# Attention scores computed transposed, softmax between 32x32 block transposes, in a fused attention and MLP kernel

## The chip, the cores and the metric

One program runs on one core of a Trainium2 chip. The metric is the device time of one execution in microseconds; lower is better.

## What is computed

The reference chains three blocks: a linear attention through 32 memory slots, a token- and channel-mixing MLP, and a gated mixture of four attention experts. The change touches only the first block and its meeting with the second:

```python
a = exp(phi - max(phi, axis=2)); a = a / (sum(a, axis=2) + 1e-09)      # over the sequence
k_m = einsum('bhsm,bhsd->bhmd', a, k); v_m = einsum('bhsm,bhsd->bhmd', a, v)
scores = matmul(q, k_m.transpose(0, 1, 3, 2)) / sqrt(64)               # 576 queries x 32 slots
attn = exp(scores - max(scores, axis=-1)); attn = attn / (sum(attn, axis=-1) + 1e-09)
attn_out = matmul(attn, v_m)
# MLP: x = heads of attn_out side by side
h = maximum(x.T @ w_tok1, 0) @ w_tok2; u = x + h.T; out = u + maximum(u @ w_ch1, 0) @ w_ch2
```

Batch 8, 8 heads, 576 positions, head size 64, 32 slots. q and k are 64 times as large as v, which is part of the inputs' setup.

## The kernel before

The attention runs in 16 units; a unit is one batch element and four heads. Each unit passes through the steps `s1a` to `s4c`, and a loop over t (lines near 560) starts the steps of several units in each round: `s1a` of unit t+3, `s2k` of t+2, `s3`, `s3b` and `s3c` of t+1, `s4a`, `s4g`, `s4b` and `s4c` of t. Between the steps it puts pieces of the channel MLP (`b1some`, tiles `b`, `u`, `uh`, `ul`, `hh`, `hl`), which fill TensorE, and pieces of the weight preparation (`go`, tiles `cst`, `cm`, `cy`), which split float64 weights on DVE and ACT. From this program text a scheduler, which models the engines' times, makes the order of each engine's queue; each queue is then executed in order.

The steps around the change:

- `s2k` (L303, L309, L312) makes the slots' keys and values: float32 products in four column tiles of 32, tile `g`, from `kv` and `ea`. `s2q` (L359, L366) turns q on TensorE into `qTb`; `s2t` turns the keys into `kmT`.
- `s3` (L376 to L383) makes the scores, tile `s` in PSUM: queries on the partitions, 4 heads x 32 slots along the row, five blocks of 128 queries (the last one half empty). DVE takes the maximum of each 32 (`smx`, L379) and subtracts it (L382, into `ssb`), ACT takes the exponential (L383).
- `s3b` (L388 to L392) sums, inverts (`ssm`), and multiplies on POOL into `at`, queries on the partitions.
- `s3c` (L402 to L405) splits `at` into a rounded part and a rest (`ahi`, `alo`) for the products with two such parts; `s4g` uses them for the token mixing's first product (L98, L434, L435, `t1h`, `t1l`).
- `s4a` (L413, L415) turns `at` on TensorE so that heads and slots lie on the partitions, and splits it into `aT`; `s4c` (L471) multiplies that with the slots' values, and adds the token mixing.

Queries lie on the partitions in the order of the load, four neighbours to a partition, and the rows of `w_tok1` are loaded in the same order (`tok1`).

Of the kernel before, what the change touches and what calls it, by code (L numbers as in the profile page):

```python
# [62 lines left out]
def fused_kernel(ctx: ExitStack, tc, q, k, v, phi, w_tok1, w_tok2, w_ch1, w_ch2,  # L63
# [136 lines left out]
    with ExitStack() as sa:  # L200
# [20 lines left out]
        qTb = [ld.tile([128, 2, 640], F32, name=f"qTb{i}") for i in range(NB2)]  # L221
        for i in range(NB2):
            DVE.memset(phb[i][64:128, :, 4, :], NEG)
            DVE.memset(qTb[i][:, :, S:640], 0.0)
# [128 lines left out]
        def s2q(n, part):  # L353
            qn = qn_
            qT = qTb[n % NB2]
            if part < 2:
# [5 lines left out]
                ACT.activation(qT[:, part, 0:512], p3[:], AF.Copy)  # L362
# [8 lines left out]
        def s3(n):  # L371
            qT, km = qTb[n % NB2], kmT.pop(n)
            p = pp.tile([128, 5, 4, M], F32, name="s", bufs=1)
            for j in range(5):
                for pr in range(2):
                    PE.matmul(p[:, j, 2 * pr:2 * pr + 2, :], lhsT=qT[:, pr, 128 * j:128 * j + 128],  # L376
                              rhs=km[:, 64 * pr:64 * pr + 64], start=True, stop=True)
            mx = wk_.tile([128, 5, 4], F32, name="smx", bufs=1)
            DVE.tensor_reduce(mx[:], p[:], axis=AX.X, op=OP.max)  # L379
            s = wk_.tile([128, 5, 4, M], F32, name="ssb", bufs=1)  # L380
            ssb[n] = s
            DVE.tensor_sub(s[:], p[:], mx[:, :, :, None].to_broadcast([128, 5, 4, M]))  # L382
            ACT.activation(s[:], s[:], AF.Exp, scale=scale)  # L383

        def s3b(n):
            s = ssb.pop(n)
            sm = wk_.tile([128, 5, 4], F32, name="ssm", bufs=2)
# [3 lines left out]
            a_ = wk_.tile([128, 5, 128], F32, name="at", bufs=1)  # L391
            POOL.tensor_mul(a_[:].rearrange("p j (h m) -> p j h m", h=4), s[:],  # L392
                            sm[:, :, :, None].to_broadcast([128, 5, 4, M]))
            ah[n] = a_

        def s3c(n):
# [4 lines left out]

            ACT.activation(hi[:, 0:4, :], a_[:, 0:4, :], AF.Copy)  # L402
            ACT.activation(hi[0:ST, 4, :], a_[0:ST, 4, :], AF.Copy)
            POOL.tensor_sub(hi[ST:128, 4, :], a_[0:ST, 4, :], f(hi[0:ST, 4, :]))
            POOL.tensor_sub(lo[:], a_[:, 0:4, :], f(hi[:, 0:4, :]))  # L405

        def s4a(n):
            a_ = ah.pop(n)
            x_ = wk_.tile([128, 2, S], F32R, name="aT", bufs=2)
            aTt[n] = x_  # L410
            p = pp.tile([128, 512], F32, name="t", bufs=2)
            for j in range(4):
                PE.transpose(p[:, 128 * j:128 * j + 128], a_[:, j, :], ident[:])  # L413
            p2 = pp.tile([128, 128], F32, name="t", bufs=2)
            PE.transpose(p2[:], a_[:, 4, :], ident[:])  # L415

            for src, cs, j in ((p[:], slice(0, 512), 4), (p2[:, 0:ST], slice(512, S), 1)):
                if n < NR:
                    split(x_[:, 0, cs].rearrange("k (p j) -> k p j", j=j),
                          x_[:, 1, cs].rearrange("k (p j) -> k p j", j=j),  # L420
                          src.rearrange("k (j p) -> k p j", j=j))
                    continue
                for c, o in ((0, 0), (1, 64)):
                    sv = src[o:o + 64, :].rearrange("k (j p) -> k p j", j=j)
                    hv = x_[o:o + 64, c, cs].rearrange("k (p j) -> k p j", j=j)
                    lv = x_[64 - o:128 - o, c, cs].rearrange("k (p j) -> k p j", j=j)
                    split(hv, lv, sv)
# [54 lines left out]
        def tok1(j, n):  # L482
            s_ = stg.tile([128, S, 2], I32, name="cst", bufs=3)[:, 0:n * T, :]
            if j < 4:
                src = w1w[0:SM].rearrange("(p j) t -> p j t", j=4)[:, j:j + n, :]
# [885 lines left out]
```

## Time and profile before

| | us |
|---|---|
| median of 3 runs | 1220.99 |
| lowest and highest run | 1220.82, 1222.42 |
| span of the profiled execution, first to last instruction | 1219.0 |
| PE busy (97% of the span) | 1180.3 |
| PE weight loads busy (91%) | 1104.3 |
| DVE busy (67%) | 812.8 |
| ACT busy (51%) | 627.3 |
| POOL busy (35%) | 429.0 |

The page gives no time of the profiled execution other than its span; the median of the runs is 2.0 us above it. Matmuls are pipelined, so their busy times overlap, and the profile models their ends: how fast a row of matmuls runs is read from their starts. One float32 matmul appears as two passes, so an instruction of the program counts twice there. A unit's number in this document counts from 0 in the order of the program.

### The profile page before, as it was taken

How to read it: one execution, taken by the hardware profiler on the slowest of the kernel's cores; microseconds unless marked ns; L12 is line 12 of the kernel's file. 1: busy time of each engine (PE TensorE's matmuls, PEld its weight loads, DVE VectorE, ACT ScalarE, POOL GpSimd, SP SyncE). 2: the span in 40 equal slices, each digit the busy share in tenths (PEclk: the TensorE clock that was granted, in tenths of full speed). 3: DMA queues.
4: the chain of work that ended last, by engine and by line, in shares of the span. 5: the costliest groups of instructions: out<-in, count | busy, mean ns of one | idle time of the engine just before them, and what ended most of it. 6: DMA issues, size and time to landing. Idle time of an engine off the chain costs nothing.

```text
span 1219.0 us, 24055 instructions
## 1 busy us (share of the span) xinstructions
PE 1180.3 (97%) x8730; PEld 1104.3 (91%) x8730; DVE 812.8 (67%) x2013; ACT 627.3 (51%) x1651; POOL 429.0 (35%) x622
## 2 busy tenths in 40 slices
PE   5789999999999999999999999999999999999998
PEld 4689999999988889899999889999999899999986
DVE  6867778886575756667566513787676667777753
ACT  3555656566453323223222212777676766777774
POOL 1432435344001112112111344555454637373331
PEclk9699999999999999999999999999999999999999
DMA  9866767654283221232123343322323333322422
GB/s 242 228 183 179 216 163 217 189 151 118 79 295 102 104 70 35 70 104 79 61 70 104 97 112 113 87 84 79 83 87 83 88 109 91 101 84 67 149 85 104
DMA packets 160917, 145.09 MB, mean 119 GB/s; under 512 B 73248, under 2 KB 128800, under 8 KB 160800
## 3 DMA queue, kind: packets, MB, share of 16 engines
q1 hardware_dynamic: 160800, 143.57, 40.5%
q8 instruction: 69, 1.13, 0.4%
q14 instruction: 48, 0.39, 0.1%
HBM read 91.10 MB, written 40.89 MB: 108 GB/s over the span
## 4 chain that ended last, share of the span: by engine, by line
PE 89%; DVE 4%; DMA 4%; ACT 1%; SPq 1%; issue 1%; POOL 0%; ACTq 0%; DVEq 0%
PE g L98 30%; PE o L98 16%; PE h L98 15%; PE b L98 8%; PE y L1143 4%; PE s L1034 3%; PE t L1098 3%; PE s L376 2%; DMA cst<-in_moe_w_ch_dram 1%; PE g L303 1%; PE s L1056 1%; DMA cst<-in_moe_w_tok_dram 1%; PE t L359 1%; PE g L471 1%; PE t L98 1%
## 5 line engine op out<-in xcount | busy, mean ns | idle before, releaser
L1079 POOL TENSOR_TENSOR a<-a,cf 128x128 f32<-128x128 f32 (+3 forms) x128 | 88.2, 722 | 71.1 <-DVE cf L1071 70.9
L98 PE MATMUL o<-hl,w2h 128*128 128x512 f32 x288 | 112.6, 391 | 0.0
L98 PE MATMUL o<-hh,w2l 128*128 128x512 f32 x288 | 112.4, 390 | 0.0
L98 PE MATMUL o<-hh,w2h 128*128 128x512 f32 x288 | 107.9, 392 | 0.0
L649 ACT ACTIVATE hh<-m 128x256 fp32r<-128x256 f32 x96 | 38.9, 415 | 110.9 <-DVE m L720 71.3
L392 POOL TENSOR_TENSOR at<-ssb,ssm 128x640 f32<-128x640 f32 x16 | 21.5, 1343 | 173.7 <-DVE ks L319 82.1
L1023 DVE CUSTOM_DVE_ANT_0 ssb<-s,cmask 128x128 f32<-128x128 f32 (+2 forms) x144 | 68.3, 482 | 20.3 <-PE s L1034 13.1
L1036 ACT ACTIVATE a<-ssb,nb 128x128 f32<-128x128 f32 (+3 forms) x128 | 71.4, 558 | 20.2 <-DVE nb L1023 14.7
L650 DVE SCALAR_TENSOR_TENSOR hl<-m,hh 128x256 fp32r<-128x256 f32 x96 | 58.2, 616 | 17.6 <-ACT hh L649 15.5
L98 PE MATMUL g<-xh,qkl 128*128 128x288 f32 x232 | 68.4, 297 | 0.0
L98 PE MATMUL g<-xl,qkh 128*128 128x288 f32 x232 | 68.4, 297 | 0.0
L98 PE MATMUL g<-xh,qkh 128*128 128x288 f32 x232 | 68.1, 300 | 0.0
L98 PE MATMUL h<-ul,w1h 128*128 128x512 f32 (+2 forms) x200 | 66.9, 334 | 0.0
L98 PE MATMUL h<-uh,w1l 128*128 128x512 f32 (+2 forms) x200 | 66.8, 334 | 0.0
L98 PE MATMUL h<-uh,w1h 128*128 128x512 f32 (+2 forms) x200 | 66.5, 333 | 0.0
L697 POOL TENSOR_TENSOR tl<-ub,th 128x512 fp32r<-128x512 f32 x12 | 18.1, 1525 | 136.3 <-ACT th L696 136.3
L98 PEld LDWEIGHTS o<-hh,w2l 128*128 128x128 f32 x288 | 54.1, 188 | 11.4
L105 DVE TENSOR_TENSOR Bl<-t,Bh 128x512 fp32r<-128x512 f32 (+1 forms) x80 | 50.4, 634 | 20.8 <-ACT Bh L102 19.9
L98 PEld LDWEIGHTS o<-hh,w2h 128*128 128x128 f32 x288 | 54.0, 188 | 10.4 <-DVE pb L745 0.9
L932 POOL TENSOR_TENSOR xl<-p,xh 128x288 fp32r<-128x288 f32 x60 | 47.6, 812 | 44.1 <-ACT xh L931 44.1
L98 PEld LDWEIGHTS o<-hl,w2h 128*128 128x128 f32 x288 | 54.1, 188 | 9.4
L682 POOL TENSOR_TENSOR ub<-ub 128x512 f32<-128x512 f32 x6 | 9.7, 1619 | 131.0 <-DVE ul L105 131.0
(335 smaller groups left out, 4383.5 us busy)
## 6 DMA issues: line engine op xcount, KB each, us to landing
cst<-in_moe_w_ch_dram SPq DMA_DIRECT2D x24, 512.0 KB, 4.8
u_d<-u SPq DMA_DIRECT2D x32, 288.0 KB, 2.2
p_d<-u SPq DMA_DIRECT2D x16, 576.0 KB, 3.3
ub<-u_d SPq DMA_DIRECT2D x9, 1024.0 KB, 5.0
pb<-p_d SPq DMA_DIRECT2D x36, 256.0 KB, 3.9
x_d<-pb SPq DMA_DIRECT2D x36, 256.0 KB, 2.6
u<-u_d SPq DMA_DIRECT2D x16, 576.0 KB, 4.0
p<-x_d SPq DMA_DIRECT2D x15, 576.0 KB, 4.0
```

The costliest lines, as they stand in the source:

```text
L98: PE.matmul(ps, lhsT=a, rhs=b, start=start and i == 0, stop=stop and i == len(seq) - 1)
L105: DVE.tensor_sub(lo, src, f(hi))
L376: PE.matmul(p[:, j, 2 * pr:2 * pr + 2, :], lhsT=qT[:, pr, 128 * j:128 * j + 128], rhs=km[:, 64 * pr:64 * pr + 64], start=True, stop=True)
L649: ACT.activation(hh, c, AF.Relu)
L650: DVE.scalar_tensor_tensor(hl, c, 0.0, f(hh), op0=OP.max, op1=OP.subtract)
L932: POOL.tensor_sub(xl[b][:, c, ss], x_, f(xh[b][:, c, ss]))
L1023: DVE.tensor_tensor_reduce(out=out, in0=p, in1=mask, scale=-scale, scalar=least, op0=OP.add, op1=OP.min, accum_out=acc)
L1034: PE.matmul(p[:, 0:W], lhsT=q_[n][:, 128 * c:128 * c + 128], rhs=kk[n][:, 0:W], start=(i == 0), stop=(i == 1))
L1036: ACT.activation(a[:, aoff[c]:aoff[c] + W], s_[:, 0:W], AF.Exp, scale=-1.0, bias=nb[:, 0:1], accum_out=sm[:, c:c + 1])
L1079: POOL.tensor_mul(x_, x_, cf[:, c:c + 1].to_broadcast([128, W]))
L1098: PE.transpose(p[:, 128 * kc:128 * kc + 128], a[:, o + 128 * kc:o + 128 * kc + 128], ident[:])
L1143: PE.matmul(p[:, lo:w], lhsT=v_[:, kc, 0, :], rhs=x, start=(i == 0), stop=(i == len(ops) - 1))
```

## The change

- `s3` multiplies the other way round: the keys `kmT` are the weights and `qTb` streams, 512 queries and then 64, each for two pairs of heads in a column tile of 64. The scores stand with heads and slots on the partitions and queries along the row, 576 instead of 640.
- DVE transposes them in blocks of 32x32 from PSUM into `ssb`, which brings the 32 slots of a head and query into one row. DVE takes the maximum, POOL (not DVE) subtracts it in SBUF, ACT takes the exponential.
- `s3b` multiplies on POOL in place, and DVE transposes the blocks back into `at`, which now has heads and slots on the partitions.
- `s3c` turns `at` on TensorE to queries on the partitions (five transposes, the last with 64 columns) and splits it from PSUM, on ACT and DVE. `s4a` no longer turns anything; it splits `at` from SBUF, on ACT and POOL.
- `s2q` writes q in natural order, and the rows of `w_tok1` are loaded in natural order, in pieces of half the length. The padding of `qTb` and its memset go.

```diff
--- before.py
+++ after.py
@@ -218,10 +218,9 @@
             DVE.memset(kmask[32 * h:32 * h + 32, h % 2, :], 1.0)
         NB2 = 2
         phb = [ld.tile([128, 4, 5, M], F32, name=f"phb{i}") for i in range(NB2)]
-        qTb = [ld.tile([128, 2, 640], F32, name=f"qTb{i}") for i in range(NB2)]
+        qTb = [ld.tile([128, 2, S], F32, name=f"qTb{i}") for i in range(NB2)]
         for i in range(NB2):
             DVE.memset(phb[i][64:128, :, 4, :], NEG)
-            DVE.memset(qTb[i][:, :, S:640], 0.0)
         kv_ = ld.tile([128, 2, 4, 5, D], F32, name="kv")
         qn_ = ld.tile([128, 5, 4, D], F32, name="qn")
         DVE.memset(kv_[ST:128, :, :, 4, :], 0.0)
@@ -359,7 +358,8 @@
                     PE.transpose(p3[:, 128 * j:128 * j + 128],
                                  qn[:, j, 2 * part:2 * part + 2, :].rearrange("p h d -> p (h d)"),
                                  ident[:])
-                ACT.activation(qT[:, part, 0:512], p3[:], AF.Copy)
+                ACT.activation(qT[:, part, 0:512].rearrange("k (p j) -> k p j", j=4),
+                               p3[:].rearrange("k (j p) -> k p j", j=4), AF.Copy)
                 return
             p4 = pp.tile([128, 2, 128], F32, name="t", bufs=2)
             for pr in range(2):
@@ -370,27 +370,29 @@
 
         def s3(n):
             qT, km = qTb[n % NB2], kmT.pop(n)
-            p = pp.tile([128, 5, 4, M], F32, name="s", bufs=1)
-            for j in range(5):
+            p = pp.tile([128, S], F32, name="s", bufs=1)
+            for cs in (slice(0, 512), slice(512, S)):
                 for pr in range(2):
-                    PE.matmul(p[:, j, 2 * pr:2 * pr + 2, :], lhsT=qT[:, pr, 128 * j:128 * j + 128],
-                              rhs=km[:, 64 * pr:64 * pr + 64], start=True, stop=True)
-            mx = wk_.tile([128, 5, 4], F32, name="smx", bufs=1)
-            DVE.tensor_reduce(mx[:], p[:], axis=AX.X, op=OP.max)
-            s = wk_.tile([128, 5, 4, M], F32, name="ssb", bufs=1)
+                    o = 64 * pr
+                    PE.matmul(p[o:o + 64, cs], lhsT=km[:, o:o + 64], rhs=qT[:, pr, cs],
+                              start=True, stop=True, tile_position=(0, o))
+            s = wk_.tile([128, S // 32, M], F32, name="ssb", bufs=1)
             ssb[n] = s
-            DVE.tensor_sub(s[:], p[:], mx[:, :, :, None].to_broadcast([128, 5, 4, M]))
+            DVE.transpose(s[:].rearrange("p k m -> p (k m)"), p[:])
+            mx = wk_.tile([128, S // 32], F32, name="smx", bufs=1)
+            DVE.tensor_reduce(mx[:], s[:], axis=AX.X, op=OP.max)
+            POOL.tensor_sub(s[:], s[:], mx[:, :, None].to_broadcast([128, S // 32, M]))
             ACT.activation(s[:], s[:], AF.Exp, scale=scale)
 
         def s3b(n):
             s = ssb.pop(n)
-            sm = wk_.tile([128, 5, 4], F32, name="ssm", bufs=2)
+            sm = wk_.tile([128, S // 32], F32, name="ssm", bufs=2)
             DVE.tensor_reduce(sm[:], s[:], axis=AX.X, op=OP.add)
             DVE.tensor_scalar_add(sm[:], sm[:], 1e-9)
             DVE.reciprocal(sm[:], sm[:])
-            a_ = wk_.tile([128, 5, 128], F32, name="at", bufs=1)
-            POOL.tensor_mul(a_[:].rearrange("p j (h m) -> p j h m", h=4), s[:],
-                            sm[:, :, :, None].to_broadcast([128, 5, 4, M]))
+            POOL.tensor_mul(s[:], s[:], sm[:, :, None].to_broadcast([128, S // 32, M]))
+            a_ = wk_.tile([128, S], F32, name="at", bufs=1)
+            DVE.transpose(a_[:], s[:].rearrange("p k m -> p (k m)"))
             ah[n] = a_
 
         def s3c(n):
@@ -398,33 +400,24 @@
             hi = wk_.tile([128, 5, 128], F32R, name="ahi", bufs=1)
             lo = wk_.tile([128, 4, 128], F32R, name="alo", bufs=1)
             al[n] = hi, lo
-
-            ACT.activation(hi[:, 0:4, :], a_[:, 0:4, :], AF.Copy)
-            ACT.activation(hi[0:ST, 4, :], a_[0:ST, 4, :], AF.Copy)
-            POOL.tensor_sub(hi[ST:128, 4, :], a_[0:ST, 4, :], f(hi[0:ST, 4, :]))
-            POOL.tensor_sub(lo[:], a_[:, 0:4, :], f(hi[:, 0:4, :]))
+            p = pp.tile([128, 512], F32, name="t", bufs=2)
+            for j in range(4):
+                PE.transpose(p[:, 128 * j:128 * j + 128], a_[:, 128 * j:128 * j + 128], ident[:])
+            p2 = pp.tile([128, 128], F32, name="t", bufs=2)
+            PE.transpose(p2[0:ST, :], a_[:, SM:S], ident[:])
+            split(hi[:, 0:4, :], lo[:], p[:].rearrange("p (j k) -> p j k", j=4))
+            ACT.activation(hi[0:ST, 4, :], p2[0:ST, :], AF.Copy)
+            DVE.tensor_sub(hi[ST:128, 4, :], p2[0:ST, :], f(hi[0:ST, 4, :]))
 
         def s4a(n):
             a_ = ah.pop(n)
             x_ = wk_.tile([128, 2, S], F32R, name="aT", bufs=2)
             aTt[n] = x_
-            p = pp.tile([128, 512], F32, name="t", bufs=2)
-            for j in range(4):
-                PE.transpose(p[:, 128 * j:128 * j + 128], a_[:, j, :], ident[:])
-            p2 = pp.tile([128, 128], F32, name="t", bufs=2)
-            PE.transpose(p2[:], a_[:, 4, :], ident[:])
-
-            for src, cs, j in ((p[:], slice(0, 512), 4), (p2[:, 0:ST], slice(512, S), 1)):
-                if n < NR:
-                    split(x_[:, 0, cs].rearrange("k (p j) -> k p j", j=j),
-                          x_[:, 1, cs].rearrange("k (p j) -> k p j", j=j),
-                          src.rearrange("k (j p) -> k p j", j=j))
-                    continue
-                for c, o in ((0, 0), (1, 64)):
-                    sv = src[o:o + 64, :].rearrange("k (j p) -> k p j", j=j)
-                    hv = x_[o:o + 64, c, cs].rearrange("k (p j) -> k p j", j=j)
-                    lv = x_[64 - o:128 - o, c, cs].rearrange("k (p j) -> k p j", j=j)
-                    split(hv, lv, sv)
+            for c, o in ((0, 0), (1, 64)) if n >= NR else ((0, None),):
+                hs_, ls_ = (slice(0, 128), slice(0, 128)) if o is None else \
+                    (slice(o, o + 64), slice(64 - o, 128 - o))
+                ACT.activation(x_[hs_, c, :], a_[hs_, :], AF.Copy)
+                POOL.tensor_sub(x_[ls_, c if o is not None else 1, :], a_[hs_, :], f(x_[hs_, c, :]))
 
         def s4g(n):
             hi, lo = al.pop(n)
@@ -482,7 +475,7 @@
         def tok1(j, n):
             s_ = stg.tile([128, S, 2], I32, name="cst", bufs=3)[:, 0:n * T, :]
             if j < 4:
-                src = w1w[0:SM].rearrange("(p j) t -> p j t", j=4)[:, j:j + n, :]
+                src = w1w[0:SM].rearrange("(j p) t -> p j t", j=4)[:, j:j + n, :]
                 SP.dma_start(s_.rearrange("p (j f) t -> p j (f t)", j=n), src)
             else:
                 for o in (0, ST):
```

Where the scheduler puts this is shown at unit 12. On PE, before, the scores are issued in two pieces around turnings of the unit ahead, and the turnings of unit 12's own weights (`at`) stand in the next round, among the next unit's scores (`g` with `t1h`: token mixing; `pmx`: maximum over the sequence):

```order
L415 MATMUL t<-ident,at 128x128
L376 MATMUL s<-kmT,qTb_116 128x64 x4
L98 MATMUL g<-t1h,ahi 128x256
L98 MATMUL g<-t1l,ahi 128x256
...
L98 MATMUL b<-hh_3804,w2h_617 128x288
L366 MATMUL t<-ident,qn 128x128 x2
L413 MATMUL t<-ident,at 128x128 x4
L376 MATMUL s<-kmT,qTb_117 128x64 x4
L98 MATMUL b<-hl_3805,w2h_617 128x288
```

Now the scores are four matmuls in one place, and the turnings of the same unit's weights come some 64 matmuls later, behind the token mixing's second product and MLP pieces and ahead of the same unit's token mixing (`qn`: turning of q; `Vh`: slot values):

```order
L302 MATMUL g<-kv,ea 32x128 x7
L311 MATMUL g<-ones,es 128x1
L377 MATMUL s<-qTb_116,kmT 64x512 x2
L377 MATMUL s<-qTb_116,kmT 64x64 x2
L268 MATMUL t<-ident,pmx 128x128
L358 MATMUL t<-ident,qn 128x128 x4
...
L98 MATMUL b<-hh_3999,w2h_612 128x288
L405 MATMUL t<-ident,at 128x128 x4
L407 MATMUL t<-ident,at 64x128
L98 MATMUL b<-hl_4000,w2h_612 128x288
L98 MATMUL b<-hh_3999,w2l_613 128x288
```

The scores' two groups stand together, and unit 12's turnings are now in the same round as its scores.

On DVE, before, from unit 12's row maximum to its reciprocal (`kr`: the slots' normalizer; `gl`: token mixing):

```order
L379 TENSOR_REDUCE smx<-s 128x20
L105 TENSOR_TENSOR aT<-t,aT 64x64
L382 TENSOR_TENSOR ssb<-s,smx 128x640
L271 TENSOR_REDUCE pmc<-t 128x1
L263 TENSOR_REDUCE pmx<-phb_115 128x128
L105 TENSOR_TENSOR gl<-g,gh 128x256
L388 TENSOR_REDUCE ssm<-ssb 128x20
```

Now, from the first block transpose to the second (`hl` with `g`: token mixing; `ea`: phi's exponential of unit 14; `ul`, `hl` with `b`: MLP):

```order
L381 STREAM_TRANSPOSE ssb<-s 128x576
L270 TENSOR_REDUCE pmc<-t 128x1
L262 TENSOR_REDUCE pmx<-phb_115 128x128
L383 TENSOR_REDUCE smx<-ssb 128x18
L445 SCALAR_TENSOR_TENSOR hl<-g,hh 128x512
L280 TENSOR_TENSOR ea<-phb_114,t 128x640
L390 TENSOR_REDUCE ssm<-ssb 128x18
L105 TENSOR_TENSOR ul_3841<-u_3450,uh_3840 128x288
L391 TENSOR_SCALAR ssm<-ssm 128x18
L105 TENSOR_TENSOR ul_3841<-u_3450,uh_3840 128x288
L392 RECIPROCAL ssm<-ssm 128x18
L179 SCALAR_TENSOR_TENSOR hl_3960<-b,hh_3959 128x288
L395 STREAM_TRANSPOSE at<-ssb 128x576
```

Two block transposes are there, the subtraction is not, and seven instructions of other steps stand between the two transposes.

On ACT the exponential of unit 12's scores (`ssb`) now stands behind those of phi and two evictions of `s4c`:

```order
L343 ACTIVATE Vd<-Vh 64x128 x2
L361 ACTIVATE qTb_117<-t 128x512
L343 ACTIVATE Vd<-Vl 64x128 x2
L281 ACTIVATE ea<-ea 128x640
L468 ACTIVATE u_3450<-g 128x288 x2
L385 ACTIVATE ssb<-ssb 128x576
L102 ACTIVATE uh_3840<-u_3450 128x288
```

It follows the maximum, the subtraction on POOL, and these three instructions.

## Rows read from the trace of the kernel before

**Rows 1.** Busy time of the engines in three stretches, granted clock, DMA share.

```profile
core 0: us, PE busy (x) PEld busy (x) DVE busy (x) ACT busy (x) POOL busy (x), PEclk, DMA share, GB/s
0.00:96.00 96.00, 69.94 (x764) 65.08 (x765) 70.66 (x149) 44.70 (x100) 28.34 (x38) 0.88 0.84 219
96.00:340.00 244.00, 244.00 (x2292) 239.32 (x2292) 175.62 (x369) 139.91 (x360) 92.60 (x150) 1.00 0.59 164
340.00:1219.00 879.00, 866.38 (x5678) 799.88 (x5676) 566.53 (x1497) 442.70 (x1193) 308.04 (x434) 1.00 0.31 96
```

**Rows 2.** Chain that ended last, 245 to 268 us: start us, us, engine, tile, line.

```profile
248.71 1.29 PE s L376 x12
...
253.88 0.84 PE s L376 x8
254.72 1.48 PE g L98 x12
...
261.39 1.58 PE b L98 x12
...
266.09 0.44 PE t L413 x4
```

**Rows 3.** Timeline of PE, 65 to 67 us: start us, us, engine, line, op.

```profile
65.05 1.30 PE L303 MATMUL g<-kv,ea 128*32 128x128 f32 x40
66.17 0.54 PE L309 MATMUL g<-ones,ea 128*32 128x1 f32 x40
```

**Rows 4.** Per-line views: L303, L309, L392; duration ns min/median/max.

```profile
L303 PE MATMUL g<-kv,ea x640: 272/273/423, 8.8 to 295.2; 128*32 128x128 f32 x160
...
L309 PE MATMUL g<-ones,ea x240: 167/170/211, 11.0 to 103.2; 128*32 128x1 f32 x120
...
L392 POOL TENSOR_TENSOR at<-ssb,ssm x16: 1264/1268/1745, 32.6 to 316.0; 128x640 f32<-128x640 f32 x16
```

**Rows 5.** Timeline of PE, 275 to 277 us.

```profile
275.20 0.27 PE L269 MATMUL t<-ident,pmx 128*128 128x128 f32 x1
275.40 1.30 PE L303 MATMUL g<-kv,ea 128*32 128x128 f32 x40
276.63 0.38 PE L312 MATMUL g<-ones,es 128*128 128x1 f32 x2
```

**Rows 6.** Groups by line and shape, 96 to 340 us: busy us, mean ns, idle before.

```profile
L105 DVE TENSOR_TENSOR ul<-u,uh 128x288 fp32r<-128x288 f32 x52 | 26.3, 542 | 7.7 <-ACT uh L102 7.5
...
L475 ACT ACTIVATE u<-g 128x288 f32<-128x288 f32 x53 | 21.0, 406 | 17.7 <-PE g L98 16.1 <-DMA p_d<-u 1.1
...
L263 DVE TENSOR_REDUCE pmx<-phb 128x128 f32<-128x640 f32 x9 | 11.8, 1315 | 0.0
...
L379 DVE TENSOR_REDUCE smx<-s 128x20 f32<-128x640 f32 x12 | 9.9, 824 | 5.2 <-PE s L376 5.1
...
L452 DVE SCALAR_TENSOR_TENSOR hl<-g,hh 128x512 fp32r<-128x512 f32 x13 | 9.0, 689 | 11.1 <-ACT hh L451 11.1
...
L383 ACT ACTIVATE ssb<-ssb 128x640 f32<-128x640 f32 x12 | 8.8, 733 | 2.6 <-DVE ssb L382 2.6
...
L281 DVE TENSOR_TENSOR ea<-phb,t 128x640 f32<-128x640 f32 x10 | 8.1, 812 | 2.9 <-PE t L277 2.8
...
L390 DVE RECIPROCAL ssm<-ssm 128x20 f32<-128x20 f32 x12 | 3.3, 277 | 0.1
...
L389 DVE TENSOR_SCALAR ssm<-ssm 128x20 f32<-128x20 f32 x12 | 2.1, 175 | 0.0
```

**Rows 7.** Timelines of DVE and POOL, 255 to 261 us.

```profile
257.00 0.28 DVE L271 TENSOR_REDUCE pmc<-t 128x1 f32<-128x128 f32 x1
257.20 1.30 DVE L263 TENSOR_REDUCE pmx<-phb 128x128 f32<-128x640 f32 x1
...
260.24 1.27 POOL L392 TENSOR_TENSOR at<-ssb,ssm 128x640 f32<-128x640 f32 x1 [9.26 <-PE t L359]
```

**Rows 8.** Timeline of PE, 20 to 45 us.

```profile
20.79 3.67 PE L376 MATMUL s<-kmT,qTb 128*128 128x64 f32 x16 [0.30 <-ACT kmT L351]
```


## The prediction

> **What bounds the kernel now.** Start with the busy time by stretch [rows 1]. Between 96 and 340 us TensorE is busy for 244.00 of 244 us at a granted clock of 1.00, which is 2.4 GHz; the view of its waits names none there. DVE has 176 us, ACT 140 and POOL 93. The first 96 us are another stage: PE 69.94 us, clock 0.88, the DMA engines 84% busy. So from unit 4 on (12 of 16 units), any time taken off PE's stream shortens the kernel, and any new wait of PE lengthens it. The chain that ended last [rows 2] says the same: in it, nothing but PE follows nothing but PE. In unit 12, for example, the scores are issued in two pieces, at 248.71 and 253.88 us, and end at 254.72. POOL starts its weighting at 260.24 [rows 7], so that it is done at 261.51; PE turns it only at 266.09 [rows 2], 4.6 us later. The softmax is hidden now. That slack is what the change spends.
>
> **The scores on PE.** Removed: ten float32 matmuls per unit, twenty passes of 64 columns, each with 128 weight columns. They take 1.29 + 0.84 = 2.13 us [rows 2], 0.107 a pass. Added: two matmuls of 512 columns and two of 64, two passes each, in two column tiles. No row shows a float32 pass of 512 columns. The nearest is the key product of 128 columns in four column tiles: a pass of 128 columns shows 273 ns and one of a single column 170 [rows 4], so 103 ns for 127 columns, and 512 columns stream in some 0.42 us. Forty such passes take 1.12 us from start to start, 28 ns each [rows 3], a quarter of 103, so that four tiles run abreast. If two do here too, the unit costs 2 x 0.42 + 2 x 0.055 = 0.95 us. Lower end: one column per cycle, as the 128x288 products have (0.132 us each [rows 2]), 0.55 us. Upper end: nothing abreast, 1.9 us. I take 0.95, the reading of the nearest row.
>
> Against it stands the change between tile shapes. From a full-width transpose to the key product passes 0.20 us instead of 0.11, and the forty passes up to the next full-width matmul take 1.23 instead of 1.12 [rows 5, 3]: 0.2 us a visit. The scores are a new visit in each unit, and in about half of the units the scheduler now cuts the key product in two, so 0.3 us. PE gains 2.13 - 0.95 - 0.3 = 0.88 us a unit, 10.6 us in 12 units. The last of the five turnings has 64 weight columns instead of 128: half of 0.11 us [rows 2], 0.6 us in all.
>
> **The chain behind the scores.** Two block transposes on DVE are new, the subtraction goes from DVE to POOL, and the turnings that feed the token mixing move from the next round to where the scheduler thinks the weights ready: the order shows unit 12's turnings behind the scores by 10 transposes, 6 matmuls of 256 columns and 48 of 288, which is 10 x 0.11 + 6 x 0.123 + 48 x 0.132 = 8.2 us of PE [rows 2]. I walk the chain by the new orders. No row shows a block transpose: the nearest is the reduction that reads the same scores, 0.824 us for 640 elements [rows 6], so 0.74 for 576; half of it and double it are the ends. POOL's passes are 1.268 x 576/640 = 1.14 us [rows 4].
> - DVE: transpose 0.74, the small maximum 0.28 and unit 15's large one 1.32 that stand between, row maximum 0.74: 3.08.
> - POOL subtracts meanwhile; on DVE stand hl 0.69 and ea 0.81 [rows 6], on ACT ea's exponential 0.73 and two evictions of 0.41, all ahead of the scores' exponential (0.66): 6.8.
> - DVE: sum 0.73, two ul of 0.54, the addition 0.18, the reciprocal 0.28: 9.1.
> - POOL multiplies, 1.14, and DVE turns back, 0.74: 10.9. Steps that follow one another on an engine start about 0.08 early [rows 7], seven times: 10.4.
>
> So PE, in order, waits 10.4 - 8.2 = 2.2 us at unit 12's turnings, with all of its stream behind them. Counted the same way, units 8, 10 and 14 leave 7.7 us for chains of about 10.9, 10.9 and 9.1: 3.2 + 3.2 + 1.4. The other units leave 10 to 12.7 us and wait for nothing. Sum 10.0 us of new waits.
>
> **What costs nothing.** DVE: out go a pass over PSUM and, from unit 6 on, four subtractions, in come two transposes and two subtractions: about equal, and it has 68 us to spare [rows 1]. ACT loses a little. POOL gets some 2 us per unit on 151 us of spare time. Splitting the turned weights for PE (two ACT copies ahead of the first) is covered by 12 or more matmuls, 1.6 us, behind the turnings; if it is late, PE waits 0.1 to 0.3 us. The eviction of q has the pattern that the weights' eviction had. The two first weight loads have pieces of half the size: within the first 30 us, taken as 0, at worst +1.
>
> **The first 96 us.** Scores at half clock: 16 passes in 3.67 us [rows 8], 4.6 us a unit; now about 2. PE has 26 us idle there, and each unit's chain grows by some 2 us (two transposes and the slower subtraction). The four units nearly balance; I take -2, between -6 and +6.
>
> **Sum.** -10.6 - 0.6 - 2 + 10.0 = -3.2 us on the span of 1219.0: 1215.8. The median of the runs is 2.0 above that span, and I carry this: 1217.8 us. Some 0.2%, 2.4 us, is about what a measurement can tell from no change.
>
> **The rivals.**
> 1. Nothing waits at the turnings: the scheduler placed them rightly, the block transposes take half of what I say and the exponential isn't queued behind the evictions. Then -13.2: 1207.8. For it: no wait of PE at all in this stage before. Against: the queues ahead of the exponential.
> 2. The tiles overlap less. Each float32 matmul is two passes on one tile; if passes start in order, the second on the first tile stands ahead of the first on the other, and of four long passes three follow one another: 3 x 0.42 + 0.16 = 1.42 us, 5.6 us less gain: 1223.4. For it: two tiles that alternate pass by pass can hide less than four. Against: 28 ns a pass [rows 3] where the passes stand in the same order. The Trainium skill, "TensorE: Matmul & The Clock Gate", section "The mechanism", has matmuls start and end strictly in program order. By that rule this rival is the case; the rows with four tiles don't decide it, as a pass of one column per cycle, in pairs, would give 28 ns too.
> 3. Slower: the chain is longer everywhere. A block transpose of float32 takes double (1.5 us each), and the POOL passes are held as in their longest case, 1.745 against 1.268 [rows 4]: 2.4 us more per unit. The four tight units wait 9.6 us more, and units 6 and 7, with 10 us of cover, 2.4 each: 14.4, 1232.2. It decides once the waits exceed the 13.2 us gained, at 3.3 us a tight unit. The Trainium skill, "SBUF — State Buffer", section "SBUF: two separate sides", says that POOL and a DVE instruction with two SBUF inputs lock each other out for a whole instruction. By that rule holds of this kind must come, the more so with two passes of POOL in the chain; the median of 1268 beside a maximum of 1745 shows that they are rare so far.
> 4. The change doesn't do what it says: the tiles run one after another, 1.9 + 0.3 us against 2.13; PE gains nothing and the waits stay: 1229.4. The 28 ns speak against it.
>
> **How the numbers follow.** Forecast 0.38, rivals 0.22, 0.18, 0.16 and 0.06. The forecast's own range is 1212 to 1223, its waits and the first 96 us being uncertain by some 5 us. 1206 to 1231 leaves out half of the first rival and most of the third. Faster: 0.21 of the forecast's 0.38, 0.21 of the first rival, 0.03 of the second: 0.45. Slower: 0.07 of the forecast, 0.08 of the second, 0.14 of the third, 0.06 of the fourth: 0.35. The same: 0.20.
>
> **What would show it.** Right: twelve score groups of about 1 us on PE after 96 us, and PE waiting at the turnings of the weights for DVE, 1 to 3 us, in units 8, 10, 12 and 14 alone. Wrong: no such waits (rival 1); groups of 1.4 us (2) or 1.9 (4); waits in nearly every unit, with block transposes above 1 us or POOL passes above 1.5 (3); or a difference that arises before 96 us or behind 340 us, where I expect none beyond 6 us.

## The result, and the profile after

The changed kernel takes 1228.96 us (median of 5 runs, 1228.62 to 1231.94) against 1220.82 us for the kernel before beside it: 1.0071 of the time, 95% interval 1.0051 to 1.0091. It is slower by some 8 us. The forecast was 1217.8; the range, 1206 to 1231, holds the time, and the side was wrong.

The profiled execution, the longest of the five, took 1231.94 us with a span of 1230.2, so 11 us more than the span of before. All of that arises ahead of the channel stage. Its first matmul (`h`) starts at 345.25 us before and at 357.25 now, 12.0 us later; what follows takes 873.7 us before and 872.9 now. Two rows of the timelines of PE, the kernel before and then the change:

```profile
345.25 0.63 PE L98 MATMUL h<-uh,w1h 128*128 128x512 f32 x2
```

```profile
357.25 0.74 PE L98 MATMUL h<-uh,w1h 128*128 128x512 f32 x2 [0.19 <-ACT uh L102]
```

The busy time by stretch of the change, cut at 96 us and at that first matmul (columns as in [rows 1]):

```profile
0.00:96.00 96.00, 68.19 (x711) 55.47 (x711) 71.41 (x146) 42.20 (x89) 26.32 (x36) 0.95 0.80 210
96.00:357.25 261.25, 250.19 (x2185) 224.67 (x2183) 182.74 (x374) 145.44 (x352) 117.14 (x162) 1.00 0.56 162
```

PE was never idle between 96 and 340 us [rows 1]; now it is for 11.1 us of this stretch. The six largest of its nine waits there (total in us, times, longest):

```profile
PE g L98 <- DVE hl L445: 4.1, 5, 1.5
PE b L98 <- DVE hl L179: 1.5, 2, 0.7
PE g L98 <- ACT ahi L102: 1.0, 2, 0.5
PE b L98 <- DVE u L187: 0.9, 2, 0.7
PE b L98 <- DVE ul L105: 0.9, 2, 0.7
PE t L405 <- DVE at L395: 0.7, 1, 0.7
```

The wait that the forecast spoke of, `at` at the turnings (L405), is the last and smallest of these rows. The largest is one that it did not speak of, for the low part of the hidden rows (`hl`, L445).

The idle column shows only half. A 288-column matmul is followed by the next after 0.13 us, but its row lasts 0.30, so a wait is counted as idle only for what exceeds those 0.17 us. I therefore took all steps from one start on PE to the next, set each beside the median step of the same pair of shapes over all runs of this case, and call what is left over delay (the starts within the key product and within the pairs of the scores are taken as they are). That splits the stretch up to the first `h` in two parts, the work and the delays:

```
                    done by 96 us | left: work  delay  sum
before                   50.0     |  242.0    7.2  249.2
the change               46.3     |  231.9   29.2  261.1
change, late turnings    47.9     |  234.4   15.9  250.3
best version (e10)       50.1     |  227.5   15.1  242.6
```

(With late turnings six matmuls of the channel block, 0.8 us, stand behind the first `h` and are not counted.) Over all 16 units PE's work fell from 292.0 to 278.2 us, 0.86 us a unit. Behind 96 us 10.1 us less work was left, and 22.0 us of delay came in its place. These are estimates: with other choices of the steps to take as they are, the figures behind 96 us move by about 1 us, those of the first column and of the whole by 2 to 3, and the gain of a unit lies between 0.75 and 0.86.

**The new operations.** The score group of unit 11 on PE, and the per-line views of the block transposes and of POOL's two passes (ns min/median/max):

```profile
252.16 1.20 PE L377 MATMUL s<-qTb,kmT 128*64 128x512 f32 x8
253.29 0.33 PE L268 MATMUL t<-ident,pmx 128*128 128x128 f32 x1
```

```profile
L381 DVE STREAM_TRANSPOSE ssb<-s x16: 760/776/784, 23.5 to 328.2; 128x576 f32<-128x576 f32 x16
...
L395 DVE STREAM_TRANSPOSE at<-ssb x16: 762/778/780, 34.7 to 335.3; 128x576 f32<-128x576 f32 x16
...
L384 POOL TENSOR_TENSOR ssb<-ssb,smx x16: 1157/1160/1470, 25.9 to 329.9; 128x576 f32<-128x576 f32 x16
...
L393 POOL TENSOR_TENSOR ssb<-ssb,ssm x16: 1151/1161/1462, 33.1 to 333.2; 128x576 f32<-128x576 f32 x16
```

From its first start to the next instruction the group takes 253.29 - 252.16 = 1.13 us, of which 0.15 is the way back to full width. Within it the eight passes start at 252.163, .170, .643, .650, 253.073, .080, .129 and .135: in pairs 7 ns apart, 0.48 us from the first long pair to the second and 0.43 from that to the first short one. Two tiles run abreast, and a pass of 512 columns takes about what the forecast gave it (0.42).

**Where the time goes in one unit.** Unit 12, the one that the forecast walked through. PE, from the scores' end to the turnings (the view begins within the scores and shows six of their eight passes):

```profile
272.00 0.71 PE L377 MATMUL s<-qTb,kmT 128*64 128x512 f32 x6
...
275.05 0.29 PE L98 MATMUL g<-t2l,hh 128*128 128x288 f32 x1
276.28 0.40 PE L98 MATMUL g<-t2h,hl 128*128 128x288 f32 x1 [0.94 <-DVE hl L445]
...
281.83 0.29 PE L98 MATMUL b<-uh,w1l 128*128 128x288 f32 x1
282.85 0.40 PE L98 MATMUL b<-hh,w2h 128*128 128x288 f32 x1 [0.73 <-DVE hl L179]
...
283.63 0.41 PE L405 MATMUL t<-ident,at 128*128 128x128 f32 x2
```

and DVE meanwhile, with one row of ACT behind it:

```profile
272.76 0.78 DVE L381 STREAM_TRANSPOSE ssb<-s 128x576 f32<-128x576 f32 x1 [0.39 <-PE s L377]
273.47 0.25 DVE L270 TENSOR_REDUCE pmc<-t 128x1 f32<-128x128 f32 x1
273.64 1.33 DVE L262 TENSOR_REDUCE pmx<-phb 128x128 f32<-128x640 f32 x1
274.87 0.76 DVE L383 TENSOR_REDUCE smx<-ssb 128x18 f32<-128x576 f32 x1
275.53 0.69 DVE L445 SCALAR_TENSOR_TENSOR hl<-g,hh 128x512 fp32r<-128x512 f32 x1
...
282.34 0.46 DVE L179 SCALAR_TENSOR_TENSOR hl<-b,hh 128x288 fp32r<-128x288 f32 x1 [1.28 <-ACT hh L178]
282.71 0.77 DVE L395 STREAM_TRANSPOSE at<-ssb 128x576 f32<-128x576 f32 x1
```

```profile
274.16 0.60 ACT L444 ACTIVATE hh<-g 128x512 fp32r<-128x512 f32 x1
```

The scores end at 272.71 and `at` at 283.48: a chain of 10.77 us, where the forecast walked to 10.4. The cover, 8.2 us of PE's steps in the forecast, is 10.9 us from the scores' end to the turnings less 3.0 of delay, 7.9. But PE doesn't stand at the turnings for the rest. It has stood before: 1.1 us at 276.28, because `hl` of unit 11 stands on DVE behind the transpose, the large maximum and the row maximum (its input was there at 274.76, it starts at 275.53, so 0.8 of the 1.1 us), and 0.9 us at 282.85 for a `hl` of the first channel block. When PE reaches the turnings, `at` has just come: it is done at 283.48, and the first turning starts 0.15 us later.

The same 0.15 us lie between `at` and the turnings in units 6, 8 and 10. In unit 8 PE stands at both places, for `hl` and again for `at`, so 0.15 us is what it takes to follow `at` where it waits:

```profile
195.47 0.40 PE L98 MATMUL g<-t2h,hl 128*128 128x288 f32 x1 [1.52 <-DVE hl L445]
...
202.12 0.63 PE L405 MATMUL t<-ident,at 128*128 128x128 f32 x4 [0.74 <-DVE at L395]
```

```profile
201.20 0.78 DVE L395 STREAM_TRANSPOSE at<-ssb 128x576 f32<-128x576 f32 x1 [1.05 <-POOL ssb L393]
```

So in units 6, 8, 10 and 12 the chain behind the scores does set when the turnings start. What PE loses there ahead of them it would otherwise lose at them, unless the earlier wait itself makes the chain later, which no run separates.

### The profile page after: what moved, and what is told of

It reads as the page before. It is cut to its first block, busy times and chain, and to the rows that moved or that the text cites. A ratio compares the mean times of both kernels' runs of the same rounds, so it can differ in the third digit from the quotient of the medians.

```text
span 1230.2 us, 23606 instructions
## 1 busy us (share of the span) xinstructions
PE 1180.8 (96%) x8538; PEld 1076.5 (88%) x8538; DVE 817.8 (66%) x2007; ACT 627.7 (51%) x1625; POOL 452.5 (37%) x632
## 4 chain that ended last, share of the span: by engine, by line
PE 82%; DVE 7%; DMA 4%; ACT 3%; issue 1%; SPq 1%; POOL 0%; DVEq 0%; ACTq 0%; POOLq 0%
PE g L98 29%; PE o L98 15%; PE h L98 15%; PE b L98 6%; PE y L1136 4%; PE s L1027 3%; PE t L1091 3%; PE g L302 2%; PE s L377 1%; PE s L1049 1%; DMA cst<-in_moe_w_ch_dram 1%; DMA ub<-u_d 1%; DVE ul L105 1%; PE t L98 1%; PE t L358 1%
## 5 line engine op out<-in xcount | busy, mean ns | idle before, releaser
L105 DVE TENSOR_TENSOR Bl<-t,Bh 128x512 fp32r<-128x512 f32 (+1 forms) x80 | 50.4, 634 | 21.8 <-ACT Bh L102 20.8
L98 PEld LDWEIGHTS o<-hl,w2h 128*128 128x128 f32 x288 | 54.1, 188 | 10.1 <-DVE hl L643 0.6
L1143 POOL TENSOR_TENSOR yl<-yt,yh 128x256 fp32r<-128x256 f32 x30 | 22.1, 737 | 91.8 <-ACT yh L1142 87.2
```

Source lines behind the costliest of these rows:

```text
L98: PE.matmul(ps, lhsT=a, rhs=b, start=start and i == 0, stop=stop and i == len(seq) - 1)
L105: DVE.tensor_sub(lo, src, f(hi))
```

## The experiments

Three theories were set against each other. **A**: PE was made so short that evictions set the pace. **B**: DVE, which works in order, is held inside the softmax's chain by the handovers to POOL. **C**: the change puts the turnings, with the mixing behind them, too close behind the scores. All ratios are against runs of the kernel before on the same chip, with 95% intervals. Each edit also makes the scheduler write a new order on every engine.

**e1: the subtraction on DVE.**

```diff
-            POOL.tensor_sub(s[:], s[:], mx[:, :, None]...)
+            DVE.tensor_sub(s[:], s[:], mx[:, :, None]...)
```

> The changed kernel with the subtraction of the row maximum back on DVE instead of POOL; all else as in the change. Theory B (DVE works in order and stands still inside the softmax's chain, 6.7 us at the row sum and 8.0 us at the turning back between 96 and 340 us, so that what is queued behind, the second part of the hidden rows first of all, comes late to PE): one handover less per unit, the waits at the row sum go (about 7 us of DVE's idle time), PE gets back 3 to 6 us: 1223 to 1226. Theory A (PE has been made short enough that the evictions set the pace, whoever does them): DVE gets 0.8 us more per unit and nothing is won: 1228 to 1232. Theory C (the turnings moved into the round are what costs): no change beyond 2 us, 1227 to 1231.

Measured: 1230.83 us, 1.0072 [1.0058, 1.0086]. DVE's standing still at the row sum fell from 6.7 to 1.9 us (the change, then e1, 96 to 340 us), and the time did not fall:

```profile
DVE ssm L390 <- ACT ssb L385: 6.7, 7, 2.2
```

```profile
DVE ssm L390 <- ACT ssb L385: 1.9, 5, 0.7
```

**e2: both passes on DVE** (L393 likewise).

> The changed kernel with both passes of the softmax that POOL has, the subtraction and the weighting, on DVE; nothing of the chain but the exponential leaves DVE then. Theory B: both kinds of standing still, 14.7 us of DVE, go; PE gets back 6 to 12 us: 1217 to 1223. Theory A: DVE has 1.6 us more per unit, some 20 us in the stage, of its 69 us of spare time, and PE waits for it more often: 1230 to 1238. Theory C: about as the change, 1227 to 1231.

Measured: 1228.44 us, 1.0052 [1.0035, 1.0069]: some 2 us less than the change by the ratios, though the two intervals overlap. Both standings still are gone from DVE's waits and most of the loss is still there. Theory B falls as the main cause, and theory A isn't borne out either: DVE has 1.6 us more per unit and nothing is lost.

**e3: the turnings a round later**, beside the splitting for the values.

```diff
             on(s4a, t)
+            on(s3c, t)
...
-            on(s3c, t + 1)
```

> The changed kernel with the turnings of the softmax weights and their splitting written one round later, beside the splitting for the values, where they stood before the change. Theory C (the turnings in the round of the scores are what costs: PE waits at them and behind them, 6.2 us with the first unit's, and the two copies and the difference for the mixing, 9.6 us of DVE's standing still, hold up the rest): most of the loss goes, 1215 to 1221. Theory B (DVE held inside the softmax's chain): the chain is the same, 1226 to 1231. Theory A: no change beyond 3 us.

Measured: 1219.60 us, 0.9986 [0.9976, 0.9995]. One moved line takes back the whole loss, 10 us less than the change, as theory C had it. From the end of the scores to the turnings pass 12 to 17 us in units 4 to 14 now (9 to 13 in the change), `at` is ready 2.7 us or more ahead of them, and the wait for `hl` L445 is gone behind 96 us. The waits of PE listed there are:

```profile
PE h L98 <- ACT uh L102: 1.6, 1, 1.6
PE t L405 <- ACT kmT L350: 0.8, 2, 0.6
PE b L98 <- DVE u L187: 0.8, 1, 0.8
PE b L98 <- DVE hl L179: 0.7, 1, 0.7
PE b L98 <- ACT hh L178: 0.4, 1, 0.4
```

**e4: in the kernel before, ten score passes in place of twenty.**

```diff
-                for pr in range(2):
-                    PE.matmul(p[:, j, 2 * pr:2 * pr + 2, :], lhsT=qT[:, pr, 128 * j:128 * j + 128],
-                              rhs=km[:, 64 * pr:64 * pr + 64], start=True, stop=True)
+                PE.matmul(p[:, j, :, :], lhsT=qT[:, j % 2, 128 * j:128 * j + 128],
+                          rhs=km[:], start=True, stop=True)
```

> The kernel before the change with ten passes of 128 columns for the scores of a unit instead of twenty of 64: it leaves out that heads 2 and 3 use their own half of q, so every token tile is multiplied with one half alone. About 1.0 us of PE per unit is taken away and nothing else. If PE sets the pace of the stage (theories B and C: what the change lost, it lost by what it added behind the scores), the time falls by 9 to 12 us: 1209 to 1212. If other engines set it as soon as PE is shorter (theory A), most of that turns into waits of PE: 1216 to 1221.

Measured: 1200.81 us, 0.9827 [0.9810, 0.9843]. PE's work fell by 18.3 us over the 16 units, and the time by 20.6 (more than expected, since the expectation counted 12 units). In the kernel before, time off PE is time off the kernel. Theory A falls there.

**d1: PE work added to the change**, 14 us that nothing needs.

```diff
-                for j in range(4):
+                for j in (0, 1, 2, 3, 0, 1, 2, 3):
                     PE.transpose(p3[:, 128 * j:128 * j + 128],
```

> The changed kernel with the eight full turnings of q of a unit issued twice, into the same place: 0.87 us more of PE per unit, 14 us in all, that no other work needs. If the changed kernel's stage is bound by the chain from the scores to the mixing (theory C: PE stands while that chain runs), the added work fills the waits, and at most half of it shows: 1229 to 1236. If PE sets the pace there too and the loss is only in its own work, all of it shows: 1241 to 1244.

Measured: 1234.70 us, 1.0112 [1.0098, 1.0125], 5 us above the change. About nine of 14 us fill delays: here PE alone no longer sets the pace. **a7: only the mixing moved**, behind the key product, with the turnings where the change has them.

```diff
-            on(s4g, t)
...
             on(s2k, t + 2)
+            on(s4g, t)
```

> The changed kernel, its turnings where the change put them, with the token mixing alone written behind the key product. If it is the distance from the turnings to the mixing that is too short in the change (1.3 to 3.8 us between the two in its trace, against 4 to 10 with late turnings), moving only the mixing heals as much as the late turnings did: 1218 to 1222. If it is the distance from the scores to the turnings and all that hangs on them (10 to 16 us in the change, 16 to 20 with late turnings: theory C), little is won: 1226 to 1231; the key product is not in one piece here (26 pieces), so nothing comes from that side.

Measured: 1224.06 us, 1.0023 [1.0011, 1.0034], between the two expectations: 6 us are won. The two distances hardly changed (1.5 to 3.4 us from the turnings to the mixing, 12 to 17 from the first score to the turnings in units 5 to 11; 2.1 to 3.8 and 12 to 14 in the change). The delay behind 96 us fell from 29.2 to 24.4, and at 96 us 3.4 us less work was left. What did change is the chain: in units 8, 10, 12 and 14 it took 9.1, 9.8, 8.7 and 7.2 us (10.7, 10.8, 10.8 and 8.5 in the change), `at` was ready 0.6 us or more ahead of the turnings in units 4 to 14, and the delay from the scores' end to the turnings in those four units fell from 11.1 to 5.2 us. So the place of the turnings isn't the only one that heals; theory C in its narrow form (that distance alone) is too simple: by these rows it is the chain's length against that distance that counts.

**Towards a better version.** e5 and e5m put both passes, or the weighting alone, on DVE with late turnings.

> The kernel with the late turnings (written a round later), with the subtraction and the weighting on DVE besides. On the change itself that took 2.4 us off. Theory C (what costs is how much of a round lies between the scores and the turnings, with a whole round PE sets the pace again): the two handovers from DVE to POOL and back are covered now, so the same as with the late turnings alone, 1218 to 1221, or a little worse, since DVE has 1.6 us more per unit. Theory B (DVE held in order by POOL, 7.8 us at the turning back and 4.9 at the row sum in the trace with late turnings): 4 us or more off, 1213 to 1216.

> The kernel with the late turnings, with the weighting alone on DVE: row sum, reciprocal, weighting and turning back follow one another on one engine, the subtraction stays on POOL. Theory C: 1218 to 1221. Theory B: the 7.8 us at the turning back go, 2 to 4 us off: 1215.5 to 1218.

Measured: 1222.89 us, 1.0016 [1.0005, 1.0027], and 1223.73 us, 1.0018 [1.0010, 1.0027]. Nothing is won, 4 us are lost, more than either theory said. Whether the new order or DVE's added work costs them, no run separates. **e7: late turnings, and the mixing behind the key product.**

> The kernel with the late turnings, with the token mixing written behind the key product, not ahead of it: PE's order then has 16 key products in one piece each, where the late turnings alone have them in 24 pieces and the kernel before in 18. Each piece more is a change of tile shape there and back, 0.2 us more than a step without one, some 0.3 to 0.4 us. If PE sets the pace again with the late turnings (theory C), 8 pieces fewer are 2.5 to 3 us: 1216 to 1217.5. If waits still set it, the later mixing moves the differences of gates and hidden rows later: 1219 to 1226.

Measured: 1218.25 us, 0.9973 [0.9964, 0.9983], 1.6 us less than e3 by the ratios, with intervals that overlap, and between the two expectations. The same edit on the kernel before, **b7**, and 14 us of needless PE work on e7, **d2**:

> The kernel before the change, with the token mixing written behind the key product, the edit that took the late turnings from 0.9986 to 0.9973 of the kernel before. PE's order has 17 key products here against 18, so by the price of a piece more (0.3 to 0.4 us) it wins nothing: 1219.5 to 1222.5. If the edit helps for another reason (the mixing's wait), it helps here too: 1217 to 1219.

> The kernel with late turnings and the mixing behind the key product, with the eight full turnings of q of a unit issued twice: the same 0.87 us of PE per unit, 14 us in all, that cost the changed kernel only some 5 us. If PE sets the pace again once a round lies between scores and turnings (theory C): 11 to 14 us more than the 1218 without, 1229 to 1232. If the chain still sets it: 1220 to 1226.

Measured: b7 1224.61 us, 1.0025 [1.0014, 1.0037], a loss that was not expected; d2 1226.68 us, 1.0035 [1.0023, 1.0047], 7.6 us above e7. About half of the added work shows, so PE's pace and the delays share the stage there.

In e7 the scores stand in two pieces, the 64-column pair behind full-width turnings. **e12** turned q's last 64 tokens ahead of the others; as written, this also loads the next unit's q ahead of the turning of the first 512 tokens, so these belong to the next unit. **e10** moves the same line behind the first 512, all of q its own. **f1** takes the tiles away.

```diff
             on(s2q, t + 2, 1)
+            on(s2q, t + 2, 2)
...
                 if i == 0:
                     on(s2t, t + 2)
-                    on(s2q, t + 2, 2)
```

> The kernel with late turnings and the mixing behind the key product, with the turning of q's last 64 tokens written ahead of the first 512, so that the scores stand in PE's order in one piece per unit (with late turnings the pair of 64 columns stands apart, behind the turnings, in nearly all units). If PE sets the pace (theory C), one visit less to the two-tile shape is worth 0.2 to 0.3 us per unit: 1213.5 to 1216. If not, 1217 to 1221.

> The kernel with late turnings and the mixing behind the key product, with the turning of q's last 64 tokens moved ahead of the value stage, right behind the first 512 (all of q its own): the scores then stand in one piece in PE's order in 15 of 16 units. If the second visit to the two-tile shape matters, 0.2 to 0.3 us per unit: 1213.5 to 1216. If waits take what is missing: 1217 to 1221.

> The kernel with late turnings and the mixing behind the key product, with the scores in full width: one matmul of 512 columns and one of 64 in place of two tiles each; it leaves out that heads 2 and 3 use their own half of q (all four use one half), so there is no change of tile shape at the scores. If a full-width pass of 512 columns takes no longer than one in a tile, only the changes of shape go, 0.2 to 0.5 us per unit with the scores in two pieces. If these set what is missing: 1212 to 1215.5. If waits take it: 1216.5 to 1220.

Measured: e12 1221.02 us, 0.9986 [0.9975, 0.9997]: no gain though the scores are in one piece. e10 1211.09 us, **0.9905 [0.9890, 0.9920]**. f1 1211.22 us, 0.9902 [0.9886, 0.9919]. Both lie below all that was expected. By f1, the order of e7 without the two-tile shape takes 8 to 9 us less, 0.5 us a unit, the upper end of what was expected for the visits; the new order that the edit brings is in this number too. e10's stretches:

```profile
0.00:96.00 96.00, 70.83 (x743) 57.80 (x744) 81.79 (x159) 47.04 (x100) 30.96 (x39) 0.89 0.86 227
96.00:338.63 242.63, 238.63 (x2152) 220.02 (x2151) 179.19 (x363) 140.17 (x343) 116.80 (x159) 1.00 0.59 169
```

The last four ask whether that line wins by itself, and what holds e10 now.

> The kernel before the change with the turning of q's last 64 tokens ahead of the value stage, right behind the first 512. Its scores have no tile shape of their own to be visited, so if the edit won by bringing the scores into one piece, nothing is won here: 1220 to 1224. If it wins by itself, 1210 to 1216.

> The changed kernel, its turnings where the change put them, with the turning of q's last 64 tokens moved likewise. If the short distance from the scores to the turnings sets the time (theory C), the edit helps little: 1225 to 1231. If the loss came from the tail of the scores being late, 1213 to 1220.

> The kernel with late turnings and the earlier turning of q's tail, the mixing where the change has it, ahead of the key product (24 key products in PE's order in place of 16 to 18). If both edits add up by their prices on PE, 2 to 3 us above the version with all three: 1213 to 1215; if the mixing's place decides, 1217 to 1221.

> The version with late turnings, mixing behind the key product and the earlier turning of q's tail, with the eight full turnings of q of a unit issued twice, 14 us of PE more. If PE sets its pace: 1223 to 1226. If waits still hide part of it, as they hid 9 of 14 us in the changed kernel and 6 of 14 in the version without the earlier tail: 1216 to 1221.

Measured: b10 1215.82 us, 0.9957 [0.9942, 0.9973]; a10 1223.24 us, 1.0020 [1.0010, 1.0031]; c10 1214.19 us, 0.9945 [0.9931, 0.9959]; d3 1214.34 us, 0.9948 [0.9933, 0.9962]. a10 lies between its two expectations, c10 where both edits add up, d3 below both of its own. The line is worth 5 to 8 us wherever it stands, in the kernel before too. There it wins in the first 96 us, where 58.9 us of PE's work are done in place of 50.0:

```profile
0.00:96.00 96.00, 75.26 (x897) 69.19 (x899) 80.04 (x162) 49.31 (x108) 29.25 (x39) 0.93 0.89 233
```

So the like-for-like comparison of the scores in tiles is with b10, not with the kernel before: c10 stands at 0.9945 beside 0.9957, no difference that these intervals show, and e10 at 0.9905, about half a per cent better. The kernel before with both lines, the tail's and the mixing's, was not run. e10 beats both kernels.

The turnings have now been moved a round later under three orders, with no other step moved beside them: 10 us came off the change (e3), 6 us off a7 (1.0023 to 0.9973, e7) and 9 us off a10 (1.0020 to 0.9945, c10). So it isn't the luck of one new order that their place makes most of the loss.

d3's added work costs 5 us of 14: delays (15.1 us) still hide part of PE's work in e10. Which order would free them was not tried.

## Why the prediction was wrong

**The scores on PE: right.** 0.88 us a unit were forecast, plus 0.05 for the 64-column turning; the work fell by some 0.8 (0.86 by the table). In detail 1.13 us stand for the group and its way back (forecast 0.95 and 0.2 for the visit), and some 0.1 for the way in. Rivals 2 and 4 fall with the pairs 7 ns apart: four long passes take 0.91 us, two after one another, not three (2) or four (4). (The fourth rival's own terms add up to 1229.2, not 1229.4.) The Trainium skill, "TensorE: Matmul & The Clock Gate", section "The mechanism", has matmuls start and end in program order; worked out pass by pass that gave 1.42 us, and the measurement decides against this reading of it for two passes on each of two column tiles.

**The new operations: right.** Block transposes took 0.776 us (0.74), POOL's passes 1.16 (1.14), POOL 117 us in place of 93 (2 us per unit). Rival 3, with its 1.5 us and its holds, falls by mechanism, though its 1232 us, like the 1229 of rival 4, lies near the time: a block transpose takes 0.78 us, not 1.5, and POOL's medians of 1160 ns beside maxima of 1470 show no general hold. Its sign "waits in nearly every unit" did come, by another way. The Trainium skill, "SBUF — State Buffer", section "SBUF: two separate sides", tells of such locking out for a whole instruction. Of the 32 passes in the change 8 took 1.27 to 1.47 us, and of the 16 in the kernel before 5 took 1.45 to 1.75, which is not as rare as the forecast read from median and maximum; whether it is this locking out, no run shows.

**The waits of the four tight units: right in size, partly wrong in place.** The chains of units 8, 10, 12 and 14 took 10.7, 10.8, 10.8 and 8.5 us (10.9, 10.9, 10.4 and 9.1 forecast). The delays of PE from the end of the scores to the turnings came to 3.4, 3.5, 3.0 and 1.3 us, 11.1 before rounding; the forecast was 10.0. But for 0.9 us at the turnings of unit 8 they stood at `hl` and at the channel block's matmuls, ahead of the turnings, so "PE waiting at the turnings in units 8, 10, 12 and 14 alone" was not to be seen.

**The step that failed** is "The other units ... wait for nothing", together with "What costs nothing". The walk asked only when the chain ends, against cover in four units, and put all else at nothing. Measured, in us of delay on PE: 11.1 in those four units, 5.0 on the same stretch in the other seven from 4 to 13, 8.7 from the turnings to the next scores in units 4 to 14, and 4.4 ahead of unit 4 and behind these. That is the 29.2 of the table; the kernel before has 7.2, so 22.0 are new against the forecast's 10.0, and the missing 12 are the difference in sign.

Three things stand in these sums. Unit 6 was a tight unit too, with a chain of 10.5 us over 9.6 of cover. Behind the turnings the first mixing matmul (`g` from `t1h` and `ahi`) waits for the split weights, 3.7 us in all behind 96 us and none in the kernel before; the forecast had "0.1 to 0.3 us" a unit beside this step and nothing in the sum. And the channel block's matmuls (`b`) come late, by the same count 10.3 us in all against 4.4 before. The wait for `hl`, which the forecast didn't ask for either, is the largest row, but 1.7, 1.4 and 1.1 us of it stand in units 8, 10 and 12, within the 11.1. How much of the channel block's delay each engine's order makes stays open. DVE's spare 68 us did not help: in unit 12 `hl` came late by its place in the queue.

**The first 96 us**: -2 forecast. The change has done 3.7 us less of PE's work there, about what four units save, so it came out at none. The first unit's turnings alone waited 5.5 us for `at`, at a place where the forecast had only a range of 6 us either way:

```profile
35.62 1.09 PE L405 MATMUL t<-ident,at 128*128 128x128 f32 x4 [5.46 <-DVE at L395]
```

The forecast's half clock for these scores is not what the view shows for the row that it reads, 1.00 at 20.8 to 24.5 us, though a pass takes 0.23 us there; from 37 to 40 us, where the view has 0.50 (1.2 GHz), 14 passes take 3.09 us, 0.22 each.

The sum again, from the span of before: 10.1 us less work left at 96 us, 22.0 us more delay, 0.8 us less behind the first `h`, makes 11 us. What the profile row of idle PE time showed of the delay was 11.1 - 0.7 = 10.4 us.

## What to carry to other kernels

When a chain of steps is put into the queue of an engine that works in order, price not only when the chain ends but also every result that now stands behind it in that queue, and who waits for it. Ask also how far a producer and its consumer stand apart on a busy engine: here one line, which moved the consumer a round later, turned 0.7% slower into 0.1% faster. And compare a change with a kernel before that has had the same new order tried: of the 12 us of the best version, the last line written alone won 5 in the kernel before as well.

## What the runs showed that was not expected

- Two float32 matmuls of 512 columns on two column tiles took 0.91 us, four passes; in full width one such matmul takes as long per pass (0.43 us from start to start in f1). The tiles double what passes through at no cost but the visit, and the visits are dear: f1, without them, won 8 to 9 us.
- A block transpose of 128x576 took 776 ns out of PSUM and 778 ns within SBUF.
- The profile's idle time of PE showed 10.4 of 22.0 us of delay, since 288-column matmuls are 0.30 us long in the records and 0.13 us apart.
- Added work of 14 us on PE cost 5.0, 7.6 and 5.2 us in three versions of the changed kernel, while taking 18.3 us off the kernel before won 20.6.
- Edits that were expected to cost nothing, and that make a new order, added 3 to 4 us (e5m, b7): about what single gains of this size amount to.
- Moving the turnings a round later won 10, 6 and 9 us under three orders of the rest.
